# A transformer prompt kernel: second tile transposed in two parts at the start, two tiles' statistics moved to ScalarE, Wk loaded ahead of the third x group, halos copied straight from the last group

## Chip, core and metric

The kernel runs on one core of a Trainium2 chip. The metric is the device time of one execution in microseconds (us), the median of several. Most executions agree within 0.1 to 0.2%. One execution of each kernel was traced.

Engines in the profile: PE is TensorE (matmul), PEld its weight loads, DVE is VectorE, ACT is ScalarE, POOL is GpSimd, SP is the engine whose queue issues most DMAs (SPq).

## The reference

Two layers, each of sliding attention and a feed-forward block, on x of 2048 rows by 1024 columns in bf16. Both layers use the same weights.

```python
x = x + A(layernorm(x), wqkv, wo)        # 32 heads of 32; each row attends to 8 rows: itself, -2, -4 ... -14
x = x + B(layernorm(x), w1, b1, w2, b2)  # gelu(x @ w1 + b1) @ w2 + b2, F = 3584
# ... and the same two lines once more
def A(x, wqkv, wo):
    q, k, v = split(x @ wqkv)
    logits = q . k[rows - 0, -2, ... -14] * scale   # rows before the first are masked
    return (softmax(logits) . v[the same rows]) @ wo
```

## The kernel before

The rows are worked in 4 groups of 512 (4 tiles of 128 rows). For each group and layer: layer norm, transposition (columns to partitions), Q, K and V by TensorE, attention by VectorE, output projection, two feed-forward matmuls. A group's attention needs the last 14 columns ("halo") of K and V of the group before. The program's names in the profile: xn is a normalised tile, xnT the same transposed, qT, kT and vT are Q, K and V, oT is the attention's output (transposed, as the output projection reads it), wt a weight tile, acc a bank of the memory that TensorE writes to; to "evict" a bank is to copy it to the working memory. TensorE is kept busy with one group's matmuls while VectorE does another's attention.

TensorE can't start before the first rows of x are loaded, normalised and transposed. To start early, the first group starts with half of its tiles: tiles 0 and 1 are transposed on TensorE, and Q is computed for these 256 columns in four rounds of two k-blocks each (a k-block is 128 of the 1024 columns that are summed over), as the four pieces of Wq arrive.

```python
load_x(0, 0, 2)                                    # tiles 0, 1
for k in range(0, KD, 2):                          # Wq in four pieces of 0.5 MB
    load_wq_piece(wq_first[k // (KD // 2)], k)
    if k < 4:
        load_x(0, 2 + k // 2, 3 + k // 2)          # tiles 2, 3 between them
...
def transpose_on_pe(xn, out, parts=None):
    pst = psum.tile([P, KD, P], BF16, name="acc", bufs=8)      # one bank
    for k in range(KD):
        pe(nc.tensor.transpose(pst[:, k, :], xn[:, k * P:(k + 1) * P], ident[:]))
    for h, copy in enumerate(parts):                           # evicted in len(parts) equal parts
        copy(out[:, h * n:(h + 1) * n, :], pst[:, h * n:(h + 1) * n, :])
...
def ln_first():
    stats(0)
    stats(1)
    xn0 = norm(0)
    xn1 = norm(1)
    transpose_on_pe(xn0, xa[0][:, 0, :, :], parts=[act.copy] * 4)
    ps = transpose_bias()
    transpose_on_pe(xn1, xa[0][:, 1, :, :], parts=[vec.tensor_copy] * 2 + [act.copy] * 2)
    warm_up(2)                                     # two matmuls on zeros
    act.copy(b1T[:], ps[:])
    stats(2)
    stats(3)
    for tt in range(2, 4):
        first_late.append((norm(tt), xa[0][:, tt, :, :]))
...
for kq in range(4):                                # in gen_qkv, first group only
    for c in range(7):
        first[c] = qkv_chunk(wq, c, xnT, first.get(c), kq * 2, (kq + 1) * 2, 0, 2)
        if (kq, c) == (2, 3):
            transpose_on_pe(*first_late.pop(0))    # tile 2
        if (kq, c) == (3, 4):
            ...
            transpose_on_pe(*first_late.pop(0))    # tile 3
```

VectorE then takes the statistics of the second and third group's eight tiles in one row, and those tiles are transposed by DMA from the same queue as the weights.

Of the kernel before, what the change touches and what calls it, by code (L numbers as in the profile page):

```python
# [17 lines left out]
def kernel(  # L18
# [123 lines left out]
            load_x(0, 2 + k // 2, 3 + k // 2)  # L142

    warm = bigp.tile([P, P], BF16, name="big")
    vec.memset(warm[:], 0.0)
    mhalf = const.tile([P, 1], F32, name="mhalf")
    pool.memset(mhalf[:], -0.5)
    eps_t = const.tile([P, 1], F32, name="eps_t")
# [4 lines left out]
    make_identity(nc, ident[:])  # L153
    mask = const.tile([P, W - 1, HALO], F32, name="mask")
    khalo = const.tile([P, NCH, HALO], BF16, name="khalo")
    vhalo = const.tile([P, NCH, HALO], BF16, name="vhalo")
    zhalo = const.tile([P, NCH, HALO], BF16, name="zhalo")
    b1T = const.tile([P, KF], F32, name="b1T")
    b2bc = const.tile([P, D], BF16, name="b2bc")
    mv_ahead = const.tile([P, NTT, 2], F32, name="mv_ahead")  # L160
    rstd_ahead = const.tile([P, NTT, 1], F32, name="rstd_ahead")

    def build_constants():
        pool.memset(zhalo[:], 0.0)
        pool.memset(mask[:], 0.0)
        first = smp.tile([H, W - 1, HALO], F32, name="z")
        pool.memset(first[:], 0.0)
        for w in range(W - 1):
            pool.memset(first[:, w, 0:HALO - DIL * w], -1e9)
        pool.dma_start(mask[0::NTT, :, :], first[:])  # L170
# [23 lines left out]
        pool.tensor_tensor(out=rstd[:], in0=rstd[:], in1=mhalf[:], op=ALU.pow)  # L194
        return mv, rstd

    def ln_stats_ahead(g):
        junk = lnp.tile([P, D], BF16, name="xn", bufs=3)
        for tt in range(NTT):
            t, mean, var = g * NTT + tt, mv_ahead[:, tt, 0:1], mv_ahead[:, tt, 1:2]  # L200
            less = lnp.tile([P, 1], F32, name="less")
            act.activation(junk[:], x[t][:], ACT.Identity, scale=-1.0 / D, accum_out=less[:])
            act.activation(junk[:], x[t][:], ACT.Square, bias=less[:], accum_out=var)
            pool.tensor_scalar(out=mean, in0=less[:], scalar1=-1.0, scalar2=None, op0=ALU.mult)
            rstd = rstd_ahead[:, tt, :]
            pool.tensor_scalar(out=rstd, in0=var, scalar1=1.0 / D, scalar2=EPS, op0=ALU.mult, op1=ALU.add)
            pool.tensor_tensor(out=rstd, in0=rstd, in1=mhalf[:], op=ALU.pow)

    def ln_norm(t, mv, rstd, xn=None):
        if xn is None:  # L210
# [1 line left out]
        vec.tensor_scalar(out=xn[:], in0=x[t][:], scalar1=mv[:, 0:1], scalar2=rstd[:], op0=ALU.subtract, op1=ALU.mult)  # L212
        return xn

    def transpose_on_pe(xn, out, parts=None):
        pst = psum.tile([P, KD, P], BF16, name="acc", bufs=8)
        for k in range(KD):
            pe(nc.tensor.transpose(pst[:, k, :], xn[:, k * P:(k + 1) * P], ident[:]))  # L218
        parts = parts or [act.copy]
        n = KD // len(parts)  # L220
        for h, copy in enumerate(parts):
            copy(out[:, h * n:(h + 1) * n, :], pst[:, h * n:(h + 1) * n, :])

    last_transpose = [None]

# [7 lines left out]
    def ln_first():  # L233

        xa[0] = new_xnT()
        vec.on = act.on = True
        mvs = {}
        stds = {}

        def stats(tt):  # L240
            st6 = lnp.tile([P, 2, 6], F32, name="stats")
            for h in range(2):
                vec.bn_stats(st6[:, h, :], x[tt][:, h * HALF:(h + 1) * HALF])
            mvs[tt] = lnp.tile([P, 2], F32, name="mv")
            vec.bn_aggr(mvs[tt][:], st6[:])
            stds[tt] = lnp.tile([P, 1], F32, name="std")
            act.activation(stds[tt][:], mvs[tt][:, 1:2], ACT.Sqrt, bias=eps_t[:])

        def norm(tt):
            rstd = lnp.tile([P, 1], F32, name="rstd")  # L250
            vec.reciprocal(rstd[:], stds[tt][:])
            return ln_norm(tt, mvs[tt], rstd)

        stats(0)
        stats(1)
        xn0 = norm(0)
        xn1 = norm(1)
        transpose_on_pe(xn0, xa[0][:, 0, :, :], parts=[act.copy] * 4)
        ps = transpose_bias()
        transpose_on_pe(xn1, xa[0][:, 1, :, :], parts=[vec.tensor_copy] * 2 + [act.copy] * 2)  # L260
        warm_up(2)
        act.copy(b1T[:], ps[:])
        stats(2)
        stats(3)
        for tt in range(2, 4):
            first_late.append((norm(tt), xa[0][:, tt, :, :]))
        vec.on = act.on = False
        act.hold()
# [38 lines left out]
    def gen_qkv(n, defer=False, qk_pool=None, v_late=False, qk_next=None, v_first=False, mix=0):  # L307
        g = n % NG
        xnT = xa.pop(n)
        s = st[n]  # L310
        s["prods"] = []
        qk_pool = qk_pool or attp
        if v_first:
            wv = load_qkv(2)
        wq = wq_first if n == 0 else load_qkv(0)
        if not v_first:
            wk = load_qkv(1)

        def values():
            vT = attp.tile([P, NCH, HALO + T], BF16, name="vT", bufs=2)  # L320
            s["vT"] = vT
            act.on = n > 2
            act.copy(vT[:, :, 0:HALO], (zhalo if g == 0 else vhalo)[:])
            act.on = False
            for c in range(NCH):
                ps = qkv_chunk(wv, c, xnT)
                act.copy(vT[:, c, HALO:], ps[:])
                yield
            if g + 1 < NG:
                act.copy(vhalo[:], vT[:, :, T:T + HALO])  # L330

        if v_first:
            yield from values()
            wk = load_qkv(1)
        if n == 0:
            early_tiles = ln_early((1, None), (2, qk_next))
            for _ in range(NTT):
                next(early_tiles)
            wv = load_qkv(2)
            for _ in early_tiles:  # L340
                pass
            load_x(3)
        qT = qk_pool.tile([P, NCH, T], BF16, name="qT")
        first = {}
        for kq in range(4 if n == 0 else 0):
            for c in range(7):
                first[c] = qkv_chunk(wq, c, xnT, first.get(c), kq * (KD // 4), (kq + 1) * (KD // 4), 0, 2)
                if (kq, c) == (2, 3):
                    transpose_on_pe(*first_late.pop(0))
                if (kq, c) == (3, 4):  # L350
                    for done in range(2):
                        act.copy(qT[:, done, 0:2 * P], first[done][:, 0:2 * P])
                    transpose_on_pe(*first_late.pop(0))
                    act.hold()
        if n == 0:
            first[7] = qkv_chunk(wq, 7, xnT, t0=0, t1=2)
        for c in list(first)[2:]:
            act.copy(qT[:, c, 0:2 * P], first[c][:, 0:2 * P])
        kT = qk_pool.tile([P, NCH, HALO + T], BF16, name="kT")
        s["qT"], s["kT"] = qT, kT  # L360
        act.on = n > 2
        act.copy(kT[:, :, 0:HALO], (zhalo if g == 0 else khalo)[:])
        act.on = False

        def query(c):
            t0 = 2 if n == 0 else 0
            ps = qkv_chunk(wq, c, xnT, t0=t0)
            act.copy(qT[:, c, t0 * P:], ps[:, t0 * P:])

        def key(c):  # L370
            ps = qkv_chunk(wk, c, xnT)
            act.copy(kT[:, c, HALO:], ps[:])
            if not defer:
                new_prod(n, c)

        ahead = mix or NCH
        turns = [(query, c) for c in range(ahead)]
        for c in range(NCH):
            turns.append((key, c))
            if ahead + c < NCH:  # L380
                turns.append((query, ahead + c))
        for i, (chunk, c) in enumerate(turns):
            if i == NCH and n > 0 and not v_late and not v_first:
                wv = load_qkv(2)
            chunk(c)
            yield
        if g + 1 < NG:
            act.copy(khalo[:], kT[:, :, T:T + HALO])
        if not v_first:
            if v_late:  # L390
                wv = load_qkv(2)
            yield from values()
# [160 lines left out]
    def warm_up(count):  # L553
        ps = acc_tile()
        for _ in range(count):
            mm(ps[:], lhsT=warm[:], rhs=warm[:].unsqueeze(1).to_broadcast([P, NTT, P]), start=True, stop=True)
# [6 lines left out]
    def ln_early(*groups):  # L563
# [5 lines left out]
            tiles += [(n * NTT + tt, xns[:, tt, :], xa[n][:, tt, :, :]) for tt in range(NTT)]  # L569
        vec.on = True  # L570
        ahead = ln_stats(tiles[0][0])
        for i, (t, xn, xT) in enumerate(tiles):
            mv_rstd = ahead
            if i + 1 < len(tiles):
                ahead = ln_stats(tiles[i + 1][0])
            ln_norm(t, *mv_rstd, xn)
            sp.dma_start_transpose(xT, xn.rearrange("s (k p) -> s k p", p=P))
            if i + 1 == len(tiles):
                vec.on = False
            yield  # L580

    def stage(gen, count=None, sides=()):

# [24 lines left out]
    build_constants()  # L608
    with tc.tile_pool(name="early", bufs=1) as early:
        load_x(1)  # L610
        load_x(2)
        stage(gen_qkv(0, qk_next=early), sides=at(14, load_b2))
        q1 = gen_qkv(1, defer=True, qk_pool=early, mix=NCH // 2)
        stage(q1, sides=at(0, gather, 0) + at(11, between, 0, 1) + at(11, hold) + each(av, 0, 12, 1))
        q2 = gen_qkv(2, defer=True)
# [57 lines left out]
```

## Time and profile before

| | before |
|---|---|
| median of the runs at prediction time | 1231.02 us (1230.63 to 1231.93) |
| span of the traced execution | 1229.1 us |
| first real matmul | 8.953 us |
| last matmul | 1225.8 us |
| VectorE's last oT of the first group | done at 124.94 us |

From the page of the kernel before: the span, the busy times, the chain of waits that ended last, and the groups of the second feed-forward matmul and of its weight loads (columns: line, engine, operation, out<-in, form, count, busy us, mean ns, idle us before).

```profile
span 1229.1 us, 13953 instructions
PE 1221.3 (99%) x5723; PEld 632.7 (51%) x5773; DVE 864.2 (70%) x918; ACT 315.1 (26%) x507; POOL 105.2 (9%) x209
...
PE acc L117 99%; DMA x<-in_A_x_dram 0%; DVE stats L92 0%; PE acc L218 0%; DVE xn L92 0%; DVE x L92 0%; DVE mv L92 0%; PE acc L181 0%; DVE rstd L92 0%
...
L117 PE MATMUL acc<-wt,hT 128*128 128x512 bf16 (+1 forms) x1780 | 386.0, 376 | 2.1
L117 PEld LDWEIGHTS <-hT 128*128 128x128 bf16 x1820 | 178.1, 98 | 209.0
```

TensorE is the bound. A busy PE row doesn't prove that it does useful work at full rate, so the starts were compared one with the next: 0.216 us for 512 columns and 0.109 us for 256. Steps of 0.43 us, twice 0.216, are scattered through the trace; the page counts 5723 matmuls and 5773 weight loads, so 50 records of matmuls are missing, and these steps are no stalls. What is left is the start. Its chain of waits (start us, us, what):

```profile
0.73 2.85 DMA x<-in_A_x_dram
3.60 1.30 DVE stats L92 x2
...
6.58 0.56 DVE xn L92
...
7.19 0.62 PE acc L218 x8
7.81 0.12 PE acc L181
7.92 0.55 PE acc L218 x8
8.48 0.43 PE acc L117 x2
...
8.95 4.12 PE acc L117 x36
```

Tile 0's eight transposes start at 7.19, the bias at 7.74, tile 1's eight at 7.86, and the two warm-up matmuls fill the time until the first real matmul at 8.95. The chain doesn't name VectorE's eviction of tile 1, because a warm-up stands between. The timeline of VectorE before shows it (start us, us, what, [idle before, ended by]):

```profile
7.24 0.55 DVE L92 TENSOR_SCALAR xn<-x,mv,rstd 128x1024 bf16<-128x1024 bf16 x1
8.52 0.49 DVE L92 COPY xnT<-acc 128x256 bf16<-128x256 bf16 x2 [0.73 <-PE acc L218]
```

The first of the two copies was ready to start only when all eight transposes into its bank had been done.

### The profile page before, as it was taken

To read this page: it belongs to the slowest core of one execution; us is meant where nothing else is said; L and a number is where in the kernel's file an instruction comes from. 1 tells how busy PE (TensorE), PEld (TensorE's weight loads), DVE (VectorE), ACT (ScalarE), POOL (GpSimd) and SP (SyncE) were. 2 spreads that over 40 slices of the span, in tenths; PEclk is the share of its full clock that TensorE was granted. 3 is DMA by queue.
4 is the path that set the end of the run, shared out by engine and by line. 5 is a ranking of instruction groups with operands and counts; after the bars stand their busy time and mean duration, and the time that the engine had idled before them with its cause. 6 is when DMAs were issued, how large, how long until landed. Compare 5 with 4: busy or idle time off the path is not lost.

```text
span 1229.1 us, 13953 instructions
## 1 busy us (share of the span) xinstructions
PE 1221.3 (99%) x5723; PEld 632.7 (51%) x5773; DVE 864.2 (70%) x918; ACT 315.1 (26%) x507; POOL 105.2 (9%) x209
## 2 busy tenths in 40 slices
PE   9999999999999999999999999999999999999998
PEld 7666544456444564446544465444654444444444
DVE  8999896998997999375993759937599797011001
ACT  4343253014410144202441024410244001400310
POOL 3010015010101101100001000010000002000000
PEclk9999999999999999999999999999999999999999
DMA  9954674756648745856557565576664558446441
GB/s 299 293 205 154 178 238 153 201 171 206 215 133 239 188 151 167 235 169 181 155 160 233 171 171 175 155 222 202 171 199 145 189 195 203 155 160 195 154 136 52
DMA packets 220031, 226.64 MB, mean 184 GB/s; under 512 B 68194, under 2 KB 187136, under 8 KB 217920
## 3 DMA queue, kind: packets, MB, share of 16 engines
q1 hardware_dynamic: 214704, 208.69, 56.9%
q0 software_dynamic: 5264, 17.06, 3.6%
q8 instruction: 45, 0.74, 0.2%
q14 instruction: 18, 0.15, 0.0%
HBM read 189.01 MB, written 4.19 MB: 157 GB/s over the span
## 4 chain that ended last, share of the span: by engine, by line
PE 99%; DVE 0%; issue 0%; DMA 0%
PE acc L117 99%; DMA x<-in_A_x_dram 0%; DVE stats L92 0%; PE acc L218 0%; DVE xn L92 0%; DVE x L92 0%; DVE mv L92 0%; PE acc L181 0%; DVE rstd L92 0%
## 5 line engine op out<-in xcount | busy, mean ns | idle before, releaser
L117 PE MATMUL acc<-xnT,wt 128*128 128x512 bf16 (+1 forms) x3392 | 720.3, 375 | 0.1
L117 PEld LDWEIGHTS <-wt 128*128 128x128 bf16 x3392 | 400.8, 119 | 318.0 <-issue 0.5
L117 PE MATMUL acc<-wt,hT 128*128 128x512 bf16 (+1 forms) x1780 | 386.0, 376 | 2.1
L117 PEld LDWEIGHTS <-hT 128*128 128x128 bf16 x1820 | 178.1, 98 | 209.0
L92 DVE TENSOR_TENSOR big<-big 128x1024 bf16<-128x1024 bf16 (+2 forms) x184 | 244.7, 1358 | 2.2
L92 ACT ACTIVATE hT<-acc,b1T 128x512 bf16<-128x512 f32 x224 | 152.1, 687 | 325.1 <-PE acc L117 325.0
L92 DVE TENSOR_TENSOR big<-qT,kT 128x4096 bf16<-128x4096 bf16 x64 | 143.8, 2284 | 36.4 <-ACT kT L92 35.9
L92 DVE TENSOR_TENSOR tmp<-acc,b2bc 128x512 f32<-128x512 f32 x56 | 38.6, 689 | 161.6 <-PE acc L117 158.5
L92 DVE TENSOR_TENSOR big<-abc,vT 128x4096 bf16<-128x4096 bf16 x64 | 144.6, 2284 | 9.8 <-DMA abc<-a 7.4
L92 ACT CAST qT<-acc 128x512 bf16<-128x512 f32 (+1 forms) x72 | 38.2, 543 | 277.6 <-PE acc L117 277.6
L117 PE MATMUL acc<-wt,oT 128*128 128x512 bf16 x440 | 97.6, 379 | 0.5
L92 DVE BATCH_NORM_STATS2 stats<-x 128x6 f32<-128x512 bf16 x120 | 79.9, 680 | 3.7 <-DMA x<-in_A_x_dram 2.7
L117 PEld LDWEIGHTS <-oT 128*128 128x128 bf16 x448 | 43.8, 98 | 53.0 <-DVE oT L92 0.3
L92 DVE TENSOR_TENSOR x<-acc,big 128x512 bf16<-128x512 f32 (+1 forms) x9 | 5.7, 632 | 90.1 <-PE acc L117 90.0
L92 ACT CAST vT<-acc 128x512 bf16<-128x512 f32 x64 | 37.4, 585 | 100.9 <-PE acc L117 100.8
L92 POOL TENSOR_TENSOR rstd<-mv,eps_t 128x1 f32<-128x1 f32 x56 | 17.4, 311 | 527.5 <-DVE mv L92 527.5
L92 ACT CAST kT<-acc 128x512 bf16<-128x512 f32 x64 | 37.3, 585 | 68.7 <-PE acc L117 68.7
L92 DVE TENSOR_TENSOR x<-acc,x 128x512 bf16<-128x512 f32 x64 | 43.0, 672 | 4.9 <-PE acc L117 4.4
L92 DVE TENSOR_SCALAR xn<-x,mv,rstd 128x1024 bf16<-128x1024 bf16 x52 | 28.4, 546 | 19.9 <-POOL rstd L92 19.5
L92 DVE TENSOR_TENSOR x<-tmp,x 128x512 bf16<-128x512 f32 x56 | 38.6, 689 | 1.4
L92 POOL DMA_DIRECT2D big<-big x24 | 13.3, 563 | 212.8 <-DVE big L92 212.8
L92 POOL TENSOR_TENSOR rstd<-rstd,mhalf 128x1 f32<-128x1 f32 x56 | 30.9, 551 | 4.4
(63 smaller groups left out, 259.4 us busy)
## 6 DMA issues: line engine op xcount, KB each, us to landing
wt<-in_B_w_dram SPq DMA_DIRECT2D x56, 1024.0 KB, 5.8
wt<-in_B_w_dram SPq DMA_DIRECT2D x64, 896.0 KB, 4.9
wt<-in_A_wqkv_dram SPq DMA_DIRECT2D x46, 1024.0 KB, 5.7
wt<-in_A_wo_dram SPq DMA_DIRECT2D x16, 1024.0 KB, 5.3
abc<-a POOLq DMA_DIRECT2D x32, 256.0 KB, 4.7
big<-big POOLq DMA_DIRECT2D x24, 256.0 KB, 3.8
x<-in_A_x_dram SPq DMA_DIRECT2D x16, 256.0 KB, 5.7
out_dram<-x SPq DMA_DIRECT2D x31, 128.0 KB, 1.8
```

What stands on the lines that cost most here:

```text
L92: inst = f(*args, **kwargs)
L117: return pe(nc.tensor.matmul(*args, **kwargs))
```

## The change

Its intent, part by part:

- **Start.** Tile 1 is normalised in 256 and 768 columns. Its first two blocks go to a bank of their own and are evicted by VectorE at once; the bias is transposed between, then the other six blocks follow. The two warm-up matmuls go.
- **Order of loads.** Wk is issued ahead of the third x group.
- **Statistics.** The last two tiles of the third group get their statistics from ScalarE and are normalised and transposed later. (A stage is cut into numbered units of work; `at(9, f)` runs f at unit 9.)
- **Halos.** V's halo, and K's in the first groups, is copied from the last group's tile itself; zero halos are memset by GpSimd. (The diff below shows V's part.)

```diff
-    vec.memset(warm[:], 0.0)
+    pool.memset(warm[:], 0.0)
...
-    def transpose_on_pe(xn, out, parts=None):
+    def transpose_on_pe(xn, out, parts):
         pst = psum.tile([P, KD, P], BF16, name="acc", bufs=8)
-        for k in range(KD):
+        for k in range(parts[0][0], parts[-1][1]):
...
-        xn1 = norm(1)
-        transpose_on_pe(xn0, xa[0][:, 0, :, :], parts=[act.copy] * 4)
+        xn1 = norm(1, (0, 2 * P, D))
+        transpose_on_pe(xn0, xa[0][:, 0, :, :], [(0, 2, act.copy), (2, 8, act.copy)])
+        transpose_on_pe(xn1, xa[0][:, 1, :, :], [(0, 2, vec.tensor_copy)])
         ps = transpose_bias()
-        transpose_on_pe(xn1, xa[0][:, 1, :, :], parts=[vec.tensor_copy] * 2 + [act.copy] * 2)
-        warm_up(2)
-        act.copy(b1T[:], ps[:])
+        transpose_on_pe(xn1, xa[0][:, 1, :, :], [(2, 8, act.copy)])
+        vec.tensor_copy(b1T[:], ps[:])
...
-            act.copy(vT[:, :, 0:HALO], (zhalo if g == 0 else vhalo)[:])
+            if g == 0:
+                pool.memset(vT[:, :, 0:HALO], 0.0)
+            else:
+                (act.copy if n > 1 else pool.tensor_copy)(vT[:, :, 0:HALO], st[n - 1]["vT"][:, :, T:T + HALO])
...
         if n == 0:
+            load_x(2)
             early_tiles = ln_early((1, None), (2, qk_next))
...
+        on_act = tiles[-2:]                # in ln_early; normalised later, by the new ln_end()
+        tiles = tiles[:-2]
...
         load_x(1)
-        load_x(2)
-        stage(gen_qkv(0, qk_next=early), sides=at(14, load_b2))
+        stage(gen_qkv(0, qk_next=early), sides=at(9, ln_stats_ahead, 2, NTT - 2) + at(11, ln_end) + at(14, load_b2))
```

More of the change, by code (lines that the diff above doesn't have):

```diff
@@ L155 @@
     khalo = const.tile([P, NCH, HALO], BF16, name="khalo")
-    vhalo = const.tile([P, NCH, HALO], BF16, name="vhalo")
-    zhalo = const.tile([P, NCH, HALO], BF16, name="zhalo")
     b1T = const.tile([P, KF], F32, name="b1T")
@@ L163, in build_constants @@
     def build_constants():
-        pool.memset(zhalo[:], 0.0)
         pool.memset(mask[:], 0.0)
@@ L195, in ln_stats, with ln_stats_ahead @@
         return mv, rstd
-    def ln_stats_ahead(g):
+    def ln_stats_ahead(g, t0=0):
+        act.on = g == 2
         junk = lnp.tile([P, D], BF16, name="xn", bufs=3)
-        for tt in range(NTT):
+        for tt in range(t0, NTT):
             t, mean, var = g * NTT + tt, mv_ahead[:, tt, 0:1], mv_ahead[:, tt, 1:2]
@@ L207, in ln_stats_ahead @@
             pool.tensor_tensor(out=rstd, in0=rstd, in1=mhalf[:], op=ALU.pow)
+        act.on = False
     def ln_norm(t, mv, rstd, xn=None):
@@ L213, in ln_norm @@
         return xn
-    def transpose_on_pe(xn, out, parts=None):
+    def transpose_on_pe(xn, out, parts):
         pst = psum.tile([P, KD, P], BF16, name="acc", bufs=8)
-        for k in range(KD):
+        for k in range(parts[0][0], parts[-1][1]):
             pe(nc.tensor.transpose(pst[:, k, :], xn[:, k * P:(k + 1) * P], ident[:]))
-        parts = parts or [act.copy]
-        n = KD // len(parts)
-        for h, copy in enumerate(parts):
-            copy(out[:, h * n:(h + 1) * n, :], pst[:, h * n:(h + 1) * n, :])
+        for k0, k1, copy in parts:
+            copy(out[:, k0:k1, :], pst[:, k0:k1, :])
     last_transpose = [None]
@@ L247, in stats, with norm @@
             act.activation(stds[tt][:], mvs[tt][:, 1:2], ACT.Sqrt, bias=eps_t[:])
-        def norm(tt):
+        def norm(tt, bounds=(0, D)):
             rstd = lnp.tile([P, 1], F32, name="rstd")
             vec.reciprocal(rstd[:], stds[tt][:])
-            return ln_norm(tt, mvs[tt], rstd)
+            xn = lnp.tile([P, D], BF16, name="xn", bufs=3)
+            for lo, hi in zip(bounds[:-1], bounds[1:]):
+                vec.tensor_scalar(out=xn[:, lo:hi], in0=x[tt][:, lo:hi], scalar1=mvs[tt][:, 0:1], scalar2=rstd[:],
+                                  op0=ALU.subtract, op1=ALU.mult)
+            return xn
         stats(0)
@@ L328, in values @@
                 yield
-            if g + 1 < NG:
-                act.copy(vhalo[:], vT[:, :, T:T + HALO])
         if v_first:
@@ L348, in gen_qkv @@
                 if (kq, c) == (2, 3):
-                    transpose_on_pe(*first_late.pop(0))
+                    transpose_on_pe(*first_late.pop(0), [(0, KD, act.copy)])
                 if (kq, c) == (3, 4):
@@ L352, in gen_qkv @@
                         act.copy(qT[:, done, 0:2 * P], first[done][:, 0:2 * P])
-                    transpose_on_pe(*first_late.pop(0))
+                    transpose_on_pe(*first_late.pop(0), [(0, KD, act.copy)])
                     act.hold()
@@ L361, in gen_qkv @@
         act.on = n > 2
-        act.copy(kT[:, :, 0:HALO], (zhalo if g == 0 else khalo)[:])
+        if g == 0:
+            pool.memset(kT[:, :, 0:HALO], 0.0)
+        else:
+            (act.copy if n > 1 else pool.tensor_copy)(kT[:, :, 0:HALO], st[n - 1]["kT"][:, :, T:T + HALO] if n < 3 else khalo[:])
         act.on = False
@@ L386, in gen_qkv @@
             yield
-        if g + 1 < NG:
+        if g + 1 < NG and n > 1:
             act.copy(khalo[:], kT[:, :, T:T + HALO])
@@ L580, in ln_early, with ln_end @@
             yield
+        ln_rest.append(on_act)
+    ln_rest = []
+    def ln_end():
+        vec.on = True
+        for tt, (t, xn, xT) in zip((NTT - 2, NTT - 1), ln_rest.pop()):
+            ln_norm(t, mv_ahead[:, tt, :], rstd_ahead[:, tt, :], xn)
+            sp.dma_start_transpose(xT, xn.rearrange("s (k p) -> s k p", p=P))
+        vec.on = False
     def stage(gen, count=None, sides=()):
```

## The prediction

> What bounds the kernel now. The page gives TensorE 99% of the span, and the chain of waits is 98.8% matmuls. Taken start to start, the timeline shows 512-column matmuls every 0.216 us and 256-column ones every 0.109 us from the first real matmul, at 8.95 us, to the last, at about 1226 us. (The Trainium skill, "TensorE: Matmul & The Clock Gate", section "Back-to-back issue gap", has N/2.4 + 2.5 ns, 0.216 us for 512 columns: the trace agrees.) The only irregular steps after 8.95 us are some fifty of about 0.43 us, twice 0.216; the groups count fewer matmuls than weight loads (1780 to 1820, 440 to 448), so these are missing records, not stalls. After the last matmul come 3 us of output and end. The change leaves stream and tail alone; it can only move the start.
>
> The start, from the timeline. x landed at 3.57 us; statistics and the first normalisation end at 7.13. TensorE transposes tile 0 from 7.19, the bias at 7.74, then waits for tile 1's normalisation (7.24 to 7.79) and transposes it from 7.86 to 8.31. VectorE's copy of tile 1's first two blocks waits for all eight transposes: 8.52 to 8.81. The first real matmul follows at 8.95. Two warm-up matmuls (0.43 us of issue) fill that wait.
>
> After the change. Tile 1's first 256 columns are normalised by about 7.5 (estimate, from 0.55 us for 1024 columns), so their two transposes follow tile 0's eight (0.056 us each) at about 7.65. VectorE's copy, from a bank of its own, starts near 7.98 and ends near 8.27 (it took 0.29). Bias and six transposes (about 0.5 us, estimate from their steps) keep TensorE busy to about 8.4. First real matmul: about 8.4, 0.5 us earlier. Its next blocks are ready: ScalarE's two 768-column copies (0.78 us each, estimate from 1.01 for 1024) end near 9.7, wanted at 9.95; the weight pieces landed at 6.7, 8.96, 10.8 and 12.2 us, wanted at 8.4, 9.95, 11.5 and 13.5.
>
> Off the path. Two tiles' statistics go from VectorE (about 1.35 us a tile) to ScalarE (four passes of about 1 us), delaying key evictions by up to 4 us; eight banks take that. VectorE's last oT for the first output projection is ready at 124.9, wanted at 125.5, a slack of 0.5 us, which the earlier TensorE uses up unless VectorE gains too; I expect about 1 us. The third x group behind Wk lands about 6 us later (near 21 to 24), just before its statistics. Dropping the warm-ups should not cool the clock: the same skill page (section "What's actually happening") has a window of 3.4 us, and the break in matmuls is 5.9 to 8.4 us; the granted clock should stay 1.00.
>
> Predicted: 1230.5 us, 0.5 us (0.04%) below 1231.02; range 1229.7 to 1231.4 (runs spread by 1.3 us). Chances: faster by over 2% 0.005, within 2% 0.985, slower 0.01.
>
> What would show it: first 256-column matmul at 8.3 to 8.55 us; no step of PE longer than its columns after it; the chain still all matmuls; VectorE's last oT of group 0 at 124.4 or before.
>
> What would make it wrong: ScalarE's longer copies arriving after 9.95; the queue blocked by the two late transposes, so that the second group's weights come late; ScalarE's passes holding up keys so that VectorE reaches the projection late; or noise in the arrival of the first x tile, as large as the gain.

## The result

| | before | changed |
|---|---|---|
| median of the runs with the result | 1231.02 us (5 runs) | 1230.21 us (5 runs, 1230.05 to 1231.13) |
| ratio | | 0.9994, 95% interval 0.998 to 1.0008 |
| span of the first traced execution | 1229.1 us | 1229.3 us |
| first real matmul | 8.953 us | 8.238 us |

The ratio is the figure for the fast runs of both kernels; it is not exactly the ratio of the medians. The time predicted, 1230.5 us, is 0.3 us from the median, inside the range. The ratio alone can't tell the gain from nothing. Over all rounds, the medians are 1230.93 us for 41 runs of before and 1230.19 us for 15 of the changed kernel (three sets of 5): about 0.7 us, 0.06%. Nine of those 15 runs are faster than the fastest of the 41 (1230.29 us). The rounds ran on several chips, and the median of before was 1231.00, 1230.76, 1230.95 and 1230.67 us in the four sets of the experiments, so medians of different sets can be compared only to about 0.3 us.

The trace is less simple. The first real matmul came 0.7 us earlier, and yet this span is the longer one. The chain of waits of the changed kernel, from 3.1 us on:

```profile
3.12 0.47 SPq L92
3.59 0.04 issue
3.63 8.57 DMA wt<-in_A_wqkv_dram
12.21 0.05 issue
12.25 1.09 PE acc L117 x8
```

The chain no longer comes from x and the transposes. It comes from the load of Wq's third piece, issued at 3.63 us and landed at 12.21. The timeline of PE of the changed kernel:

```profile
7.02 0.74 PE L217 MATMUL acc<-ident,xn 128*128 128x128 bf16 x10 [1.05 <-DVE xn L92]
7.69 0.18 PE L178 MATMUL acc<-ident,abc 28*128 28x28 bf16 x1
7.86 0.51 PE L217 MATMUL acc<-ident,xn 128*128 128x128 bf16 x6
8.24 1.72 PE L117 MATMUL acc<-xnT,wt 128*128 128x256 bf16 x14
10.21 1.75 PE L117 MATMUL acc<-xnT,wt 128*128 128x256 bf16 x14 [0.25 <-DMA wt<-in_A_wqkv_dram]
12.25 1.09 PE L117 MATMUL acc<-xnT,wt 128*128 128x256 bf16 x8 [0.29 <-DMA wt<-in_A_wqkv_dram]
```

and of VectorE:

```profile
7.07 0.73 DVE L92 TENSOR_SCALAR xn<-x,mv,rstd 128x256 bf16<-128x256 bf16 x2
7.80 0.29 DVE L92 COPY xnT<-acc 128x256 bf16<-128x256 bf16 x1
```

Ten transposes run in one row, the copy starts at 7.80 instead of 8.52, the first matmul follows at 8.24: the start does what it was meant to. But the fourteen matmuls of a round now run dry twice, until the second and the third piece of Wq land. (The page's idle times, 0.25 and 0.29, leave out what is modelled as the pipeline's drain; from start to start the two gaps lost 0.42 and 0.46 us, and 0.06 us each in the step after.) The pieces landed at 10.16 and 12.21 us here, against 8.96 and 10.81 in the trace of before. Was that the change's doing, or chance?

### The profile page after: what moved, and what is told of

Read it like the earlier page. It is cut to its first block, busy times and chain, and to the rows that moved or that the text cites. A ratio compares the mean times of both kernels' runs of the same rounds, so it can differ in the third digit from the quotient of the medians.

```text
span 1229.3 us, 13951 instructions
## 1 busy us (share of the span) xinstructions
PE 1221.1 (99%) x5721; PEld 632.6 (51%) x5771; DVE 861.6 (70%) x912; ACT 315.5 (26%) x497; POOL 119.6 (10%) x217
## 4 chain that ended last, share of the span: by engine, by line
PE 99%; DMA 1%; issue 0%; SPq 0%; DVE 0%
PE acc L117 98%; DMA wt<-in_A_wqkv_dram 1%; SPq L92 0%; PE acc L217 0%; DVE x L92 0%
## 5 line engine op out<-in xcount | busy, mean ns | idle before, releaser
L92 DVE TENSOR_TENSOR big<-abc,vT 128x4096 bf16<-128x4096 bf16 x64 | 144.6, 2284 | 10.8 <-DMA abc<-a 6.7
L92 DVE BATCH_NORM_STATS2 stats<-x 128x6 f32<-128x512 bf16 x116 | 77.4, 681 | 8.2 <-DMA x<-in_A_x_dram 7.2
L92 DVE TENSOR_SCALAR xn<-x,mv,rstd 128x1024 bf16<-128x1024 bf16 (+2 forms) x53 | 28.6, 540 | 20.1 <-POOL rstd L92 19.9
```

Of the source, the lines that this page charges most:

```text
L92: inst = f(*args, **kwargs)
```

## The experiments

All kernels gave correct results. Four of the twelve changed the kernel further to move a suspected wait; three repeat before and after. One table serves them all. "x" is the landing of the first x tile, "first" the first real matmul, "3rd piece" the landing of Wq's third piece; "waits" is what the steps of PE behind the first matmul lost against their columns (steps over 0.03 us, without the double steps of missing records), up to 20 us and later. All are from the one traced execution; the median is that of the timed runs.

| kernel | x | first | first - x | 3rd piece | waits to 20 us | later waits | span | median |
|---|---|---|---|---|---|---|---|---|
| before | 3.57 | 8.95 | 5.38 | 10.81 | 0.03 | 0.20 | 1229.07 | 1231.02 |
| base_again | 3.41 | 8.78 | 5.37 | 11.13 | 0.03 | 0.04 | 1228.74 | 1230.93 |
| rest_only | 3.62 | 9.00 | 5.38 | 12.20 | 0.23 | 0 | 1229.15 | 1230.97 |
| start_only | 3.62 | 8.45 | 4.83 | 11.17 | 0.03 | 0.49 | 1228.86 | 1230.67 |
| changed | 3.41 | 8.24 | 4.83 | 12.21 | 0.99 | 0.19 | 1229.33 | 1230.21 |
| whole_again | 3.46 | 8.29 | 4.83 | 12.05 | 0.81 | 0.08 | 1229.07 | 1230.14 |
| whole_third | 3.24 | 8.06 | 4.82 | 11.20 | 0.18 | 0 | 1228.13 | 1230.18 |
| old_halo | 3.66 | 8.49 | 4.83 | 12.07 | 0.60 | 0 | 1229.02 | 1230.57 |
| x_first | 3.53 | 8.36 | 4.83 | 11.53 | 0.23 | 0.07 | 1228.56 | 1230.33 |
| stats_on_vec | 3.54 | 8.37 | 4.83 | 11.54 | 0.19 | 2.98 | 1231.47 | 1232.88 |
| pieces2 | 3.39 | 8.22 | 4.83 | 11.32 | 1.00 | 0.05 | 1229.15 | 1231.11 |
| pieces3 | 3.45 | 8.39 | 4.94 | cut in two | 0.99 | 0 | 1229.21 | 1230.84 |
| pieces3_x_first | 3.45 | 8.28 | 4.83 | cut in two | 0.75 | 1.27 | 1230.15 | 1231.04 |

In every row span = first + waits + 1219.9 us, within 0.07 us. The 1219.9 us are the matmuls themselves and the tail, the same in all these kernels. So a span is explained by two things: when the first matmul came, and where the stream ran dry.

### Before and after, once more

No edit. The theory (A): the waits at the start are the landing of Wq's pieces, and those landings differ from execution to execution. The rival (B): the changed order of queue or banks makes the waits, whenever the pieces land.

> The kernel before, unchanged, for a second trace and the noise. Ratio to before 1.000 within 0.001. Theory A (arrival of weights): the first 256-column matmul stays at 8.8 to 9.1 us; pieces of Wq may land up to 1.3 us later or earlier than in the first trace (6.7, 8.96, 10.8, 12.2 us), and the stream stalls only if the second lands after 10.5 or the third after 12.0, by at most 0.3 us. Theory B (the two profiled runs differ only by chance in nothing that repeats): landings agree with the first trace within 0.2 us.

> The changed kernel, unchanged, for a second trace. Both theories: first 256-column matmul at 8.2 to 8.45 us. Theory A: whatever stalls follow, each ends within 0.1 us after a piece of Wq lands, and the sum of first matmul plus stalls explains the span to 0.1 us (span = first matmul + stalls + 1220.0, from the traces: 1229.1 - 8.95 = 1220.1 before and 1229.3 - 8.24 - 0.99 = 1220.1 after). Median 0.2 to 0.8 us below before. Theory B (the 0.5 us stalls come from the new order of queue or banks): stalls of about 0.5 us at the second and third pieces again, whenever the pieces land.

Before gave 1230.93 us and no wait over 0.04 us. The changed kernel gave 1230.14 us, with waits of 0.24 and 0.42 us that ended 0.05 us after its second and third piece landed (10.03 and 12.05 us). That still fits both theories: three traces with the new load order (the third is rest_only, below) had late pieces, three without had early ones. A third look at the same changed kernel separated them:

> The changed kernel a third time, for one more trace and the spread. Theory A: span = first matmul + stalls + 1219.9 within 0.05 us again; first matmul 8.2 to 8.4; the stalls are 0.9 us if the third piece of Wq lands near 12.1 us, and under 0.2 us if it lands before 11.4. A stall at the first output projection only if PE comes there earlier than VectorE's last oT.

Here the third piece landed at 11.20 us, the loss shrank to 0.18 us and the execution took 1229.91 us. Its timeline of PE has no idle time behind the first matmul; compare the rows of 14, 14 and 8 matmuls above with the one of 36:

```profile
6.85 0.74 PE L217 MATMUL acc<-ident,xn 128*128 128x128 bf16 x10 [0.83 <-DVE xn L92]
7.52 0.18 PE L178 MATMUL acc<-ident,abc 28*128 28x28 bf16 x1
7.69 0.51 PE L217 MATMUL acc<-ident,xn 128*128 128x128 bf16 x6
8.06 4.27 PE L117 MATMUL acc<-xnT,wt 128*128 128x256 bf16 x36
```

Same program, same order, no idle time: rival B as stated is out. (In this trace all 5771 matmuls were recorded, as many as weight loads, and no step of 0.43 us is left, which confirms that those are missing records.) The fifteen times of the changed kernel fit this too: nine lie between 1229.89 and 1230.21 us and six between 1230.80 and 1231.95. With 1.8 us between time and span, the nine leave 8.2 to 8.5 us for first matmul and waits together. Of the fifteen, three were traced: one of the nine (1229.91) and two of the six, so for the others early or late pieces are inferred from the time. One of the six took 1231.95 us; it was not traced, and nothing here says why.

The data rate tells where the pieces were late. Two stretches of the start: before, changed (late pieces), whole_third (columns: window, its length, busy time of PE, PEld, DVE, ACT, POOL with counts, granted clock, DMA share, GB/s):

```profile
5.50:7.50 2.00, 0.91 (x9) 0.41 (x8) 1.89 (x7) 0.29 (x1) 0.00 (x0) 1.00 0.96 355
7.50:12.00 4.50, 4.46 (x45) 3.86 (x43) 3.67 (x11) 2.30 (x9) 0.00 (x0) 1.00 1.05 394
```

```profile
5.50:7.50 2.00, 0.95 (x12) 0.48 (x10) 1.89 (x8) 0.29 (x1) 0.00 (x0) 1.00 0.80 225
7.50:12.00 4.50, 4.21 (x40) 3.54 (x37) 3.30 (x8) 2.07 (x4) 0.00 (x0) 1.00 1.05 392
```

```profile
5.50:7.50 2.00, 1.17 (x13) 0.59 (x11) 1.89 (x7) 0.29 (x1) 0.00 (x0) 1.00 0.94 354
7.50:12.00 4.50, 4.50 (x44) 4.23 (x43) 3.99 (x12) 2.36 (x5) 0.00 (x0) 1.00 1.05 386
```

From 7.5 us on, all run at nearly the same rate. Between 5.5 and 7.5 us it is 355 or 225 GB/s. This difference is 0.26 MB in 2 us, which takes about 0.7 us at 392 GB/s (an estimate from these lines); the third piece came 1.0 us later in the changed kernel's first trace than in whole_third. So the rate explains a part, not all: old_halo, below, had 288 GB/s and its third piece at 12.07 us, stats_on_vec 271 GB/s and 11.54.

A weaker form of rival B remains: that the new order of loads makes late pieces likelier. In the seven traces with Wk ahead and Wq's pieces in their original order, the third piece landed at 11.20 to 12.21 us, in the four with the third x group ahead at 10.81 to 11.53. But SyncE's queue issues the same twelve transfers in the same order in both; the first that differs is the thirteenth, issued at 8.97 us or later. By then the first piece of Wq had landed (at 6.71 to 8.12 us), and the third followed the first by 4.06 to 4.12 us in ten of these eleven traces (4.30 in x_first). So the pieces are late before the orders differ; whether the parting of the two sets is chance stays open.

### Which part of the change does it

start_only is the kernel before with the new start alone; rest_only is the whole change with the old start.

```diff
 # start_only: before, with this from the change (and transpose_on_pe, GpSimd's memset)
+        transpose_on_pe(xn1, xa[0][:, 1, :, :], [(0, 2, vec.tensor_copy)])
         ps = transpose_bias()
+        transpose_on_pe(xn1, xa[0][:, 1, :, :], [(2, 8, act.copy)])
```

> The kernel before with only the new start (tile 1 in 256 and 768 columns, two banks, bias between, no second warm-up, warm tile zeroed by GpSimd). Theory A (all of the gain is the start): first 256-column matmul at 8.2 to 8.45 us, as in the whole change; time within 0.3 us of the whole change. Theory C (the rest of the change carries part of the gain): at least 0.4 us slower than the whole change, with stalls of PE near 24 us (Wk late) or near 125 us (last oT late).

> The whole change with the old start. Theory A: first 256-column matmul at 8.9 to 9.1 us, no stall after it but for late pieces of Wq, time within 0.3 us of the kernel before. Theory C: 0.3 us or more below the kernel before although the first matmul is as late as there.

rest_only took 1230.97 us, as before, with the first matmul as late as before: by itself the rest is worth nothing. start_only moved the first matmul by as much as the whole change (first - x is 4.83 in both) but took 1230.67 us. Its PEld timeline from 20 us on shows what theory C had in mind:

```profile
19.87 4.07 PEld L117 LDWEIGHTS <-wt 128*128 128x128 bf16 x35
24.34 27.40 PEld L117 LDWEIGHTS <-wt 128*128 128x128 bf16 x128 [0.40 <-DMA wt<-in_A_wqkv_dram]
52.29 3.66 PEld L117 LDWEIGHTS <-wt 128*128 128x128 bf16 x18 [0.54 <-DMA wt<-in_A_wqkv_dram]
```

TensorE, now earlier, meets the second half of Wk at 24 us (landed 24.30) and the second half of the second group's Wq at 52 us (landed 52.25) before they are there, and loses 0.17 and 0.32 us, nearly all of its 0.55, in this one trace (the median was 0.33 us below that of before in the same rounds, and 0.53 above the changed kernel's). In the two traces of before these loads landed in time, at 23.86 and 24.12, and at 51.04 and 51.48. So neither theory alone is right: the whole gain is made at the start, and with the rest of the change it was not lost at the next loads (no trace of the changed kernel has a wait there). Next, the rest one part at a time.

x_first is the whole change with the third x group issued ahead of Wk again, as before.

```diff
-            load_x(2)
             early_tiles = ln_early((1, None), (2, qk_next))
...
         load_x(1)
+        load_x(2)
```

> The whole change, but the third x group issued ahead of Wk again. Theory D (moving Wk ahead is what keeps the earlier TensorE fed): Wk lands 2.7 us later than in the whole change (near 21.3 and 24.0 us), its second half is wanted near 24.3, so PE stalls there, 0.1 us if the pieces of Wq land early and not at all if they had already held PE up; as a gain, VectorE's first product starts near 26 us instead of 28.2, and the last oT of group 0 is done near 123.5 instead of 124.9. Theory E (the order of the two loads does nothing): no stall at 24 us and the last oT where it was. Time within 0.4 us of the whole change either way.

There was no wait at 24 us: Wk's second half landed at 23.92 us. The time, 1230.33 us, is that of the whole change within its spread (0.43 us below before in the same rounds). VectorE's first product started at 26.10 us as expected, and its last oT of the first group was done at 124.25 us, not as early as 123.5. So in this execution the order of the loads did nothing for TensorE. It is a guard for a late execution, which came up by itself further below, in pieces3_x_first: there Wk's second half landed at 25.95 us with this order, and TensorE lost 1.27 us.

stats_on_vec is the whole change with all tiles' statistics on VectorE and all transposes in one row.

```diff
-        on_act = tiles[-2:]
-        tiles = tiles[:-2]
...
-        stage(gen_qkv(0, ...), sides=at(9, ln_stats_ahead, 2, NTT - 2) + at(11, ln_end) + at(14, load_b2))
+        stage(gen_qkv(0, ...), sides=at(14, load_b2))
```

> The whole change, but the last two tiles' statistics and transposes in one row with the others, on VectorE. Theory D: the transposes of all four tiles sit ahead of the second group's weights in the queue again, so Wq of the second group lands at 51 to 52.2 us and PE stalls there by 0.1 to 0.5 us if it comes to it early (it did 0.32 us in the start alone); VectorE's last oT about 0.5 to 1 us later than in the whole change, and a stall at the first output projection of as much as PE is then early. Theory E: no stall at 51 us; time within 0.1 us of the whole change.

It took 1232.88 us, slower than both kernels. The PEld timeline from 36 to 56 us:

```profile
38.98 12.72 PEld L117 LDWEIGHTS <-wt 128*128 128x128 bf16 x60 [1.12 <-DMA wt<-in_A_wqkv_dram]
52.17 0.64 PEld L117 LDWEIGHTS <-wt 128*128 128x128 bf16 x4 [0.47 <-DMA wt<-in_A_wqkv_dram]
54.88 1.07 PEld L117 LDWEIGHTS <-wt 128*128 128x128 bf16 x6 [2.07 <-DMA wt<-in_A_wqkv_dram]
```

Theory D expected the wait at 52 us; the other two are larger. With the third x group behind Wk, its four tiles come late to VectorE, its first product starts at 31.1 us instead of 26.5 to 28.3, and the four DMA transposes hold back the second group's Wq behind them in the queue: its halves landed at 52.13 and 54.84 us, and at 45.79 and 49.11 in whole_again. (The wait before 39 us is for the second half of Wv, landed at 38.94 instead of 36.28.) VectorE's last oT came at 127.23 us. So the two late tiles belong with the new load order: Wk ahead is paid for by taking two of the delayed tiles out of the row.

old_halo is the whole change with the halos as before.

```diff
-            if g == 0:
-                pool.memset(vT[:, :, 0:HALO], 0.0)
-            else:
-                (act.copy if n > 1 else pool.tensor_copy)(vT[:, :, 0:HALO], st[n - 1]["vT"][:, :, T:T + HALO])
+            act.copy(vT[:, :, 0:HALO], (zhalo if g == 0 else vhalo)[:])
... (and the same for K)
```

> The whole change with the halos as before (zero and halo copies by ScalarE, through the two small tiles). Theory A: nothing to see, the time within 0.3 us of the whole change and the same relation, span = first matmul + stalls + 1219.9; no stall of PE that follows a halo copy. Theory C (the halos carry a part of the gain): 0.3 us or more slower, with a wait of VectorE for kT or vT or a stall of PE near 25, 60 or 90 us that the whole change does not have.

It took 1230.57 us, 0.4 us more than the whole change in its own rounds, just over the limit set for theory A (before took 1230.67 in old_halo's rounds, and the whole change was not run in them), and none of its five times (1230.46 to 1230.86) is in the changed kernel's faster group. But its trace has nothing that follows a halo copy: the only waits are at 9.9 and 11.6 us, for the second and third piece (landed 10.04 and 12.07), and after 20 us there is none. So the trace gives the halos no part in the time; whether five late executions in a row are chance stays open.

### What makes the pieces late, and can it be helped

GpSimd issues two small loads in the first 4 us, the bias rows and the mask. no_pool_dma moves both behind 25 us.

```diff
-    pool.dma_start(b1_rows[:], B_b1.rearrange("(j p) -> j p", p=P))      # at the start
+    def load_bias(): ...                                                   # at unit 14 of the first stage
+    def bias_late(): ps = transpose_bias(); act.copy(b1T[:], ps[:])        # at unit 20
...
-        pool.dma_start(mask[0::NTT, :, :], first[:])
+        return lambda: pool.dma_start(mask[0::NTT, :, :], first[:])        # at unit 15
```

> The whole change, with GpSimd's two loads of the first 4 us (bias rows, mask) moved behind 25 us, and the bias transposed late. Theory F (those loads are what slows the queue to 150 to 300 GB/s between 3.5 and 7 us): the stretch goes, the pieces of Wq land about 1 us earlier (near 6.5, 8.6, 10.6, 12.0), no stall behind the first matmul, all executions near 1229.9. Theory G (something else slows it): the slow stretch stays and the stalls with it; first matmul at most 0.1 us earlier.

The slow stretch stayed: 214 GB/s from 3.5 to 5.5 us and 300 from 5.5 to 7.5, the third piece at 11.80 us. So the stretch comes without those two loads too (theory F is out), and its cause stays open. The kernel itself failed, at 1235.82 us: the late bias load landed at 49.5 us and its transposition, in PE's program order, held TensorE for 3.4 us. A side show of it: the matmuls behind that gap took 0.43 us a step for 3 us. From its windows:

```profile
50.00:53.00 3.00, 3.00 (x9) 1.28 (x8) 2.97 (x2) 0.00 (x0) 0.00 (x0) 0.58 1.39 324
53.00:56.00 3.00, 3.00 (x15) 2.01 (x14) 3.00 (x2) 1.17 (x2) 0.00 (x0) 1.00 0.67 139
```

The granted clock was 0.58 in that stretch (0.5 for 3.41 us, from 49.13 on), after a pause of 3.58 us between two matmuls. The Trainium skill, "TensorE: Matmul & The Clock Gate", section "What's actually happening", has half clock after an idle window of about 3.4 us; this trace is near that (the clock fell 3.17 us after the last matmul before the gap had started), and one gap can't tell the window more closely. It is also why this kernel is not in the table: its span has another 1.55 us beside first matmul and waits: 1.43 from the slow steps, 0.13 from the bias's late transposition.

The other way is to reorder what is loaded. pieces2 puts the second piece ahead of x tile 2 and the third ahead of tile 3 (the loop is written out here as single calls).

```diff
     load_wq_piece(wq_first[0], 0)
+    load_wq_piece(wq_first[0], 2)
     load_x(0, 2, 3)
-    load_wq_piece(wq_first[0], 2)
+    load_wq_piece(wq_first[1], 4)
     load_x(0, 3, 4)
-    load_wq_piece(wq_first[1], 4)
     load_wq_piece(wq_first[1], 6)
```

and normalises tile 2 before tile 3's statistics, with both tiles' transposes later on PE.

> The whole change with the second piece of Wq ahead of x tile 2 and the third ahead of tile 3, tile 2 normalised before tile 3's statistics, and their transposes half a round later on PE. Theory A (the stalls at 9.7 and 11.7 us are the landing of these pieces): they land about 0.67 us earlier than in the whole change, and the stalls shrink by 0.5 to 0.9 us in an execution with late landings; first matmul unchanged at 8.2 to 8.35; median 0.2 us below the whole change or better and less spread. If the stalls stay at these places with the pieces landed before, Theory A is wrong.

The waits for weights went as theory A said: 0.06 us at both places, with the pieces at 9.18 and 11.32 us. But the time was not lower, 1231.11 us. The timeline of PE shows why:

```profile
8.22 4.90 PE L117 MATMUL acc<-xnT,wt 128*128 128x256 bf16 x42
...
15.40 0.61 PE L219 MATMUL acc<-ident,xn 128*128 128x128 bf16 x8 [0.25 <-ACT xnT L92]
15.84 1.04 PE L117 MATMUL acc<-xnT,wt 128*128 128x256 bf16 x8
17.10 1.14 PE L117 MATMUL acc<-xnT,wt 128*128 128x256 bf16 x9 [0.22 <-ACT xnT L92]
```

Tile 3, now behind the third piece, landed at 12.00 us, and VectorE had its statistics at 14.06. ScalarE, whose instructions the program keeps in their order here, had to take tile 3's square root (14.15) before it could evict tile 2 (14.35 to 15.35), and tile 3's transposes waited for that eviction, as their line says. Then tile 3's own eviction was late. From start to start, 0.42 and 0.38 us were lost. Part of this is my order on ScalarE; the rest, as I read it, is that some 3 MB must arrive in this stretch, and moving one load forward moves another back.

pieces3 cuts the third piece in two around tile 3, and evicts tile 3 in two halves; pieces3_x_first is the same with the third x group ahead of Wk.

```diff
-    load_wq_piece(wq_first[1], 4)
+    load_wq_piece(wq_first[1], 4, 1)
     load_x(0, 3, 4)
+    load_wq_piece(wq_first[1], 5, 1)
     load_wq_piece(wq_first[1], 6)
```

> The whole change with Wq's second piece ahead of x tile 2, its third cut into two around x tile 3, tile 2 normalised before tile 3's statistics, the two late transposes later on PE, tile 3's evicted in two halves. Theory A: no stall over 0.15 us up to 17 us, so PE comes to the first output projection 0.5 to 0.8 us earlier than in the whole change's late executions; VectorE is not earlier there (124.8 to 125.0), so it waits for the last oT instead, 0.4 to 0.8 us, and the time stays within 0.3 us of the whole change. If PE does not wait there, 0.5 us faster than the whole change's slower executions.

> The same with the third x group ahead of Wk again (the order of before). Theory A: VectorE does not wait for that group, its last oT is done near 124.2 to 124.6, and PE's wait there is under 0.4 us; Wk's second half lands near 24 us, wanted near 24.2, so at most 0.2 us there. Best of all kernels: 1229.9 to 1230.1, with little spread.

Both failed to beat the change. In pieces3 (1230.84 us) the loads came slowly again (the first piece at 8.35 us), and TensorE lost 0.24 us at 12.2 us, for the other half of the third piece, and 0.47 at 15.4, for the same eviction of tile 2 behind tile 3's square root (tile 3 landed at 11.79). VectorE's last oT at 124.98 caused no wait. pieces3_x_first (1231.04 us) lost 0.52 us at the transposes of tile 3 and the 1.27 us for Wk told above. None of the variants beats the changed kernel.

## Why the prediction was right, and where it was not

**The time: right.** 1230.5 us was predicted and 1230.21 measured. Three sets of rounds gave medians of 1230.14 to 1230.21. Of the four signs that the prediction named, the first trace showed none: the first matmul came at 8.24 us, just ahead of 8.3 to 8.55, steps were longer than their columns, the chain ran through a load, and VectorE's last oT was not done by 124.4.

**The start: right, in place and size.** "First real matmul: about 8.4, 0.5 us earlier." The first matmul depends on when the first x tile lands, which varied from 3.24 to 3.66 us between traces. Counted from there it came after 5.37 to 5.38 us in all three traces with the old start, and after 4.82 to 4.83 us in all but one with the new: 0.55 us. At the landing of the old trace (3.57) that is 8.40 us, the figure predicted. Of the 0.71 us between the first two traces (8.95 - 8.24), 0.16 is an earlier landing of x and 0.55 the change. The granted clock stayed 1.00 without the two warm-ups.

**"Its next blocks are ready": half wrong; the step that failed.** ScalarE's copies were in time (they ended at 9.45, estimated 9.7). The weights were not. The prediction compared one execution's landings (8.96, 10.8) with the times wanted (9.95, 11.5) and took margins of 1.0 and 0.7 us for safe. The landings themselves move by more: the third piece came between 10.81 and 12.21 us in the eleven traces with these pieces in their original order. Before, this piece was wanted at 12.04, and the latest of these landings missed that by 0.17 us (rest_only, with the old start, lost 0.23 us); the change takes that cushion away. So the gain is 0.55 us less what the weights take back: 0.18 us in the early execution traced, 0.60, 0.81 and 0.99 in late ones. That the median came out near the prediction is in part luck: the prediction had no such term, and the median falls among the nine shorter times of 15; had two more of them been long ones, it would have been about 1230.8 us.

**VectorE: wrong.** "I expect about 1 us": its last oT moved from 124.94 to 124.90 us in the first trace. The prediction saw that the third x group would come later, "just before its statistics". It came 7.7 us later (first tile 23.27 instead of 15.55), after VectorE wanted it. The waits of VectorE between 15 and 125 us, before and changed (us in total, times, longest):

```profile
DVE big L92 <- DMA abc<-a: 2.0, 1, 2.0
DVE qT L92 <- POOL rstd L92: 0.7, 1, 0.7
```

```profile
DVE stats L92 <- DMA x<-in_A_x_dram: 2.0, 1, 2.0
DVE big L92 <- DMA abc<-a: 1.4, 1, 1.4
DVE qT L92 <- POOL rstd L92: 0.7, 1, 0.7
```

The new 2.0 us wait for x eats the relief. In the two other traces of the changed kernel the last oT was done at 124.80 and, in whole_third, where x was earlier, at 123.85 us, 1.1 us earlier than before.

**The slack at the first output projection: misread.** "Its last oT is ready at 124.9, wanted at 125.5." It was wanted at 124.88. The timeline of PEld before:

```profile
124.02 0.74 PEld L117 LDWEIGHTS <-oT 128*128 128x128 bf16 x4
125.08 0.96 PEld L117 LDWEIGHTS <-oT 128*128 128x128 bf16 x5 [0.32 <-DVE oT L92]
```

TensorE did wait there, 0.20 us (0.415 from start to start, less 0.216). Among fifty steps of 0.432 us this one of 0.415 was taken for a missing record too. The page had the right entry, and the prediction explained it away. The lesson is to check such a step against the weight loads, whose records are complete.

**Not foreseen: the rest of the change is worth nothing alone, and a part of it is needed all the same.** The prediction treated it as "off the path". start_only shows that an earlier TensorE meets the next two loads, and lost 0.49 us to them. With two tiles' statistics moved, the second of these loads landed earlier (at 49.11 us in whole_again and 49.44 in x_first, which has the old order of Wk and x, against 52.25 in start_only and 54.84 in stats_on_vec). That Wk's new place is needed was seen in one execution of another kernel only (pieces3_x_first).

**The danger named, "the queue blocked by the two late transposes", was real but small.** The load behind them (Wk's second half for the second group) landed at 58.80 us instead of 56.47; no step of PE near there was longer than its columns.

**ScalarE:** four passes of 1.06 to 1.16 us, as estimated; the third key eviction moved from 29.25 to 30.61 us, well under the 4 us allowed for.

## What to carry to other kernels

When the bounding engine's stream is unbroken, write the span as "first useful instruction + waits + constant" and check the sum on several traces: it shows a gain of half a microsecond that five timed runs of each kernel can't. Before moving a consumer forward, compare its margin with the spread of the loads over several executions and not with one trace, and look at the loads behind the next one as well. When a step gets earlier, what looked like idle reordering elsewhere may be what lets it keep its gain, so undo parts from the whole as well as adding them to the old kernel.

## What the Trainium skill lacked or had wrong

- "TensorE: Matmul & The Clock Gate", section "Back-to-back issue gap", gives about 131 ns a matmul for N=512 in a sustained stream of weight loads and matmuls, and 216 ns for an isolated one. Here the sustained stream, one weight load to each matmul, took 216 ns a step from 24 us to 1224 us, but for the waits told above and the stretch of no_pool_dma at half clock; 131 was never seen. The formula that the prediction cites from this section is the one for the isolated matmul.
- "DMA: Bandwidth & Descriptors", section "Bandwidth", has no word of a slow beginning. In this kernel the queue moved 225 to 355 GB/s between 5.5 and 7.5 us, differently in each execution, and 386 to 398 from 7.5 to 12 us, in all traces with Wq's pieces in their original order. Without GpSimd's two loads it was 300 GB/s, in one trace; the cause is open.
- "SBUF — State Buffer", section "Who interferes with whom", says that a VectorE instruction with two SBUF inputs contends with a GpSimd instruction that reads SBUF, and gives no sizes for tiny operations. Here GpSimd's power of 128x1 took 0.55 us in the kernel before, and 2.62 us in the changed one, where it runs beside VectorE's products and sums of 128x4096. That fits the rule; no run isolated it. The timeline of POOL, before and changed:

```profile
27.56 0.55 POOL L92 TENSOR_TENSOR rstd<-rstd,mhalf 128x1 f32<-128x1 f32 x1
```

```profile
32.87 2.62 POOL L92 TENSOR_TENSOR rstd_ahead<-rstd_ahead,mhalf 128x1 f32<-128x1 f32 x1
```

  It cost nothing in this kernel, but the six small operations of the two tiles took 12.3 us, and the load of b2 behind them was issued at 42.2 us instead of 28.1.
- "Perfetto Trace Analysis" does not say that some matmul records may be missing from a trace: 50 of 5773 in before and 50 of 5771 in the changed kernel's first trace were, in steps of twice the pitch (0.43 us), and 50 in each of x_first, stats_on_vec, pieces2 and no_pool_dma; none in the other eight.
